# Block 0: the V product widened tile by tile and half by half, its weights in quarters, three Q and K slabs sent from ScalarE, two tiles turned by DMA

## The chip, the cores and the metric

One core of one Trainium2 chip. The views call its engines PE (matmuls), DVE (vector), ACT (ScalarE), POOL (GpSimd) and SP (SyncE, which here only sends DMAs). The metric is the time of one execution in microseconds of the device (us), the median of several executions. The kernel before takes 1619.12 us (3 runs, 1619.05 to 1619.46). The span given by a profile is usually 1.7 to 1.8 us shorter than the execution's time, so spans are compared with spans and times with times.

## The reference, cut to what matters

Two pairs of layers, each pair one attention layer over a sliding, dilated window and one gated feed-forward layer, on x of 2048 x 1024 in bf16:

```python
def _A_ref(x, wqkv, wo):                 # D = 1024, 32 heads
    qkv = (x @ wqkv)...                  # wqkv: 1024 x 3072, Q | K | V
    ...                                  # 8 keys at distance 2 per query, softmax
    return o... @ wo
x = x + _A_ref(_layernorm(x), A_wqkv, A_wo)
x = x + _B_ref(_layernorm(x), W_gate, W_up, W_down)     # and the same two lines once more
```

Only the first microseconds matter here: the layer norm of the first 512 tokens, called block 0 (four tiles of 128 tokens), and its product with the V weights, `v = layernorm(x) @ wqkv[:, 2048:3072]`.

## The kernel before

The kernel works in blocks of 512 tokens. It turns the normalised tokens before PE multiplies them, so that the 1024 features (8 chunks of 128, the contraction, `kc`) lie on partitions. For block 0 it does this on PE: a matmul with the identity into PSUM, then a copy. Loads go out from SyncE (queue q1) in program order; two x loads go out from ScalarE (queue q10).

```python
def load_x(b):
    for t in range(b * TPB, (b + 1) * TPB):
        if t == 0: ...                                   # half from SyncE, half from ScalarE
        elif t == 2: nc.scalar.dma_start(x_tiles[t][:], ...)
        else: sp_dma(x_tiles[t][:], ...)
load_x(0)                                                # all four x tiles, ahead of any weights

def want_v(key, mid, end):                               # V weights: two slabs of 1 MB, by output columns
    for g in range(2):
        want((key, g), wqkv_v[:, :, 2 * D + g * SLAB:2 * D + (g + 1) * SLAB], ...)

# ln_first(), its order of work, cut:
    bn(0, 0); bn(0, 1); aggr(0); ...                     # statistics of tile 0 on DVE
    apply(0); turn(0); apply(1)                          # turn: 8 transposes on PE
    copy(0, "a", 1); copy(0, "a", 0); turn(1); ...
    hold["later"] = {2: (lambda: (turn(2), copy(2, "a", 0), copy(2, "v", 1))),
                     4: (lambda: (turn(3), copy(3, "v", 0), copy(3, "a", 1)))}

def v_first(ln):                                         # V of block 0: two tiles at a time, whole contraction
    plan = [(c, 0, 2) for c in range(6)] + [(c, 2, 4) for c in range(6)] + [(c, 0, 4) for c in range(6, KC)]
    ...
            for kc in range(KC):
                mm(acc[:, cols], lhsT=slab[("v0", c // 4)][:, kc, ...], rhs=ln["xnT"][:, t0:t1, kc, :], ...)
            tail_act[0] = nc.scalar.copy(st["vT"][:, c, cols], acc[:, cols]).ins
            if i in ln["later"]: ln["later"][i]()        # tiles 2 and 3 turned on PE between products
```

The weights live in a ring of five slabs of 1 MB, so the sixth (the second half of K) can only be sent when the first V slab has been used up.

## Time and profile before

| | before |
|---|---|
| time, median | 1619.12 us |
| span of the profiled execution | 1617.5 us |
| PE busy, granted clock | 1608.1 us (99%), 1.00 |
| first V product starts | 9.83 us |
| first Q product starts (V is done) | 24.83 us |

The kernel is bound by PE from end to end; PE's only long wait is at the start. The chain of waits of the kernel before in its first 30 us (columns: start in us, length in us, what the end of the span hangs on at that time):

```profile
...
2.20 7.59 DMA w_v<-in_A_wqkv_dram
9.79 0.05 issue
9.83 2.79 PE acc_v L132 x24
12.63 0.45 PE tp L358 x8
13.07 1.75 PE acc_v L132 x16
14.82 0.45 PE tp L358 x8
15.27 9.57 PE acc_v L132 x72
24.83 1.73 PE acc_q L132 x8
...
```

Everything after 9.83 us is PE. The reader should see one DMA, the first V slab, issued at 2.20 and landed 7.59 us later, and then V without a gap, with two groups of eight transposes (0.45 us each) among the products.

PE's waits in the whole kernel before (columns: who waited for whom, us in total, times, longest):

```profile
...
PE scratch L132 <- DVE ones L290: 1.5, 1, 1.5
PE acc_v L132 <- DMA w_v<-in_A_wqkv_dram: 0.9, 1, 0.9
PE tp L358 <- DVE xn_first L106: 0.7, 1, 0.7
PE tp L358 <- DVE mean L106: 0.4, 1, 0.4
```

None of them comes after 9.83 us, and PE makes up 99% of the whole chain: every microsecond that PE idles later is counted as lost.

### The profile page before, as it was taken

How to read it: one execution, taken by the hardware profiler on the slowest of the kernel's cores; microseconds unless marked ns; L12 is line 12 of the kernel's file. 1: busy time of each engine (PE TensorE's matmuls, PEld its weight loads, DVE VectorE, ACT ScalarE, POOL GpSimd, SP SyncE). 2: the span in 40 equal slices, each digit the busy share in tenths (PEclk: the TensorE clock that was granted, in tenths of full speed). 3: DMA queues.
4: the chain of work that ended last, by engine and by line, in shares of the span. 5: the costliest groups of instructions: out<-in, count | busy, mean ns of one | idle time of the engine just before them, and what ended most of it. 6: DMA issues, size and time to landing. Idle time of an engine off the chain costs nothing.

```text
span 1617.5 us, 18722 instructions
## 1 busy us (share of the span) xinstructions
PE 1608.1 (99%) x7505; PEld 784.1 (48%) x7554; DVE 1138.3 (70%) x963; ACT 475.8 (29%) x971; POOL 176.1 (11%) x164
## 2 busy tenths in 40 slices
PE   9999999999999999999999999999999999999999
PEld 6646544444444445444454444544445444444444
DVE  6999979996989698929489293893939939311211
ACT  4853311131116313603136031361313311131110
POOL 2300100010003002300053000530005100000000
PEclk9999999999999999999999999999999999999999
DMA  9868867697669767794747948479574884755452
GB/s 295 184 197 251 213 173 244 182 213 206 209 189 216 202 183 216 188 248 144 229 160 202 240 152 230 153 203 254 160 231 155 207 240 156 209 171 167 155 169 66
DMA packets 408440, 317.92 MB, mean 197 GB/s; under 512 B 166432, under 2 KB 389024, under 8 KB 407840
## 3 DMA queue, kind: packets, MB, share of 16 engines
q1 hardware_dynamic: 407776, 316.13, 69.4%
q8 instruction: 59, 0.97, 0.2%
q10 hardware_dynamic: 576, 0.59, 0.1%
q14 instruction: 29, 0.24, 0.1%
HBM read 266.29 MB, written 34.66 MB: 186 GB/s over the span
## 4 chain that ended last, share of the span: by engine, by line
PE 99%; DMA 0%; issue 0%; SPq 0%; DVE 0%; DVEq 0%
PE acc_u L132 24%; PE acc_g L132 24%; PE dacc L132 18%; PE acc_v L132 7%; PE acc_q L132 7%; PE acc_k L132 7%; PE acc_wo L132 7%; PE dacc_pair L132 6%; DMA w_v<-in_A_wqkv_dram 0%; PE tp L358 0%; SPq L121 0%; PE L L132 0%; DVE x L778 0%; SPq L118 0%; DVEq L1017 0%
## 5 line engine op out<-in xcount | busy, mean ns | idle before, releaser
L132 PE MATMUL acc_g<-xnT_b,w_g 128*128 128x512 bf16 x1792 | 423.3, 379 | 0.0
L132 PE MATMUL acc_u<-xnT_b,w_u 128*128 128x512 bf16 x1792 | 423.3, 379 | 0.0
L731 ACT ACTIVATE r<-acc_g 128x512 bf16<-128x512 f32 x224 | 133.6, 596 | 728.7 <-PE acc_g L132 703.8
L106 DVE TENSOR_TENSOR hT<-acc_u,r 128x512 bf16<-128x512 f32 x224 | 151.0, 687 | 243.3 <-PE acc_u L132 240.8
L132 PE MATMUL dacc<-w_d,hT 128*128 128x512 bf16 (+1 forms) x1372 | 300.4, 375 | 1.5
L132 PEld LDWEIGHTS <-hT 128*128 128x128 bf16 x1820 | 178.1, 98 | 209.0
L132 PEld LDWEIGHTS <-w_g 128*128 128x128 bf16 x1792 | 175.4, 98 | 211.4
L132 PEld LDWEIGHTS <-w_u 128*128 128x128 bf16 x1792 | 175.3, 98 | 211.4
L106 DVE TENSOR_TENSOR pv<-a,vhm 128x4096 bf16<-128x4096 bf16 x64 | 143.6, 2285 | 0.0
L778 DVE TENSOR_TENSOR x<-dacc,x 128x512 bf16<-128x512 f32 (+1 forms) x38 | 24.5, 673 | 154.1 <-PE dacc L132 154.1
L549 DVE TENSOR_TENSOR t<-q,k 128x2048 f32<-128x2048 bf16 x56 | 128.0, 2292 | 6.7 <-ACT k L485 4.6
L106 DVE TENSOR_TENSOR t<-q,k 128x2048 f32<-128x2048 bf16 x56 | 127.5, 2287 | 3.9 <-ACT k L485 2.4
L106 DVE TENSOR_TENSOR pv<-pv 128x1024 bf16<-128x1024 bf16 (+1 forms) x128 | 113.8, 952 | 0.0
L132 PE MATMUL acc_wo<-w_o,oT 128*128 128x512 bf16 x498 | 111.1, 379 | 0.7
L249 POOL TENSOR_TENSOR st_b<-st_b,neg_half 128x1 f32<-128x1 f32 x29 | 43.8, 1517 | 609.9 <-ACT st_b L248 609.9
L562 DVE TENSOR_TENSOR ac<-ac,t 128x2048 f32<-128x2048 f32 x48 | 109.7, 2285 | 0.3
L106 DVE TENSOR_TENSOR ac<-ac,t 128x2048 f32<-128x2048 f32 x48 | 109.7, 2285 | 0.0
L490 POOL COPY kh<-k 128x14 bf16<-128x14 bf16 x40 | 53.7, 1348 | 506.5 <-ACT k L485 410.4
L132 PE MATMUL dacc_pair<-w_d,hT 128*128 128x512 bf16 x413 | 95.5, 379 | 0.4
L132 PEld LDWEIGHTS <-oT 128*128 128x128 bf16 x512 | 50.1, 98 | 60.4
L244 ACT ACTIVATE xn_b<-x 128x1024 bf16<-128x1024 bf16 x29 | 30.3, 1047 | 128.6 <-DVE x L106 66.5
L410 ACT CAST vT<-acc_v 128x512 bf16<-128x512 f32 x56 | 32.7, 586 | 54.0 <-PE acc_v L132 54.0
(131 smaller groups left out, 1226.8 us busy)
## 6 DMA issues: line engine op xcount, KB each, us to landing
w_g<-in_B_W_gate_dram SPq DMA_DIRECT2D x56, 1024.0 KB, 7.2
w_u<-in_B_W_up_dram SPq DMA_DIRECT2D x56, 1024.0 KB, 5.5
w_d<-in_B_W_down_dram SPq DMA_DIRECT2D x48, 1024.0 KB, 6.0
w_o<-in_A_wo_dram SPq DMA_DIRECT2D x16, 1024.0 KB, 6.6
vhm<-v_d SPq DMA_DIRECT2D x32, 284.0 KB, 6.7
v_d<-vT SPq DMA_DIRECT2D x8, 1024.0 KB, 9.0
oT<-o_d SPq DMA_DIRECT2D x32, 256.0 KB, 4.5
w_d<-in_B_W_down_dram SPq DMA_DIRECT2D x16, 512.0 KB, 3.7
```

The source lines that it names most:

```text
L106: tail_dve[0] = f(*args, **kwargs).ins
L132: tail_pe[0] = nc.tensor.matmul(*args, **kwargs).ins
L244: nc.scalar.activation(xn, xt[:], ACT.Square, accum_out=sq)
L249: nc.gpsimd.tensor_tensor(rstd, vpe, neg_half[:, 0:1], op=ALU.pow)
L410: tail_act[0] = nc.scalar.copy(st["vT"][:, c, :], acc[:]).ins
L490: nc.gpsimd.tensor_copy(khalo[n][:, c, :], k[:, BLK:BLK + HALO])
L549: nc.vector.tensor_tensor(t[:], i0, i1, op=ALU.mult)
L562: nc.vector.tensor_tensor(o, ac[:], t[:], op=ALU.add)
L731: tail_act[0] = nc.scalar.activation(rs[j][:], acc[:], ACT.Relu).ins
L778: run = dv if n < NB - 2 else (lambda f, *args, **kwargs: f(*args, **kwargs))
```

## The change

The intent is to start V earlier. V is widened tile by tile (first tile 0 alone, then tile 1) and its contraction is taken in two halves, so that the first products need only tile 0 and a quarter of the V weights. The V slabs are cut by contraction rows and each is sent as two DMAs of 512 KB; x tile 3 goes behind the first V slab. Three slabs of 1 MB go out from ScalarE: the first Q half (`act_slab("q", 0)`), the second Q half and the first K half. Tiles 2 and 3 are turned by DMA (SBUF to SBUF, issued by SyncE) instead of on PE, which also saves the PSUM copies. Smaller parts: the variance term goes from DVE to POOL, block 0 makes Q ahead of K by two groups, and the head sums move with it.

```diff
-    load_x(0)
+    load_x(0, range(TPB - 1))
...
+    def want_v_first(end0, end1):
+        for hh, end in enumerate((end0, end1)):
+            want(("v0", hh), qkv_half(2, hh), end)
...
+        if key[0] == "v0":
+            for i in range(2):
+                rows = slice(i * (KC // 4), (i + 1) * (KC // 4))
+                start(tv[:, rows, :], src[:, rows, :])
...
+    load_slab(("v0", 0), qkv_half(2, 0))
+    load_x(0, [TPB - 1])
+    load_slab(("v0", 1), qkv_half(2, 1))
...
+        def act_slab(nm, hh):
+            def start(dst, src):
+                on("a", nc.scalar.dma_start, dst, src)
+            load_slab(("qk01", nm, hh), qkv_half("qk".index(nm), hh), start)
+
+        def turn_dma(t):
+            return lambda: sp_dma(hold["xnT"][:, t, :, :], xna[:, t, :], True)
...
+        copy(0, "a", 0)
+        act_slab("q", 0)
...
+        def second():
+            turn(1)
+            apply(2)
+            copy(1, "v", 0)
+            copy(1, "v", 1)
+            act_square(3)
+            act_mean(3)
+            act_slab("q", 1)
+            act_slab("k", 0)
+            act_power(3)
+            apply(3)
...
-        hold["later"] = {2: (lambda: (turn(2), ...)), 4: (lambda: (turn(3), ...))}
+        hold["turns"] = [turn_dma(2), turn_dma(3)]
...
-        plan = [(c, 0, 2) for c in range(6)] + [(c, 2, 4) for c in range(6)] + [(c, 0, 4) for c in range(6, KC)]
+        tail = [(GRP * (2 + 4 * part + 0.5 * i), second_half(i, 2 * part)) for part in range(2) for i in range(KC // 2)]
+        return head, [(GRP, first_half(1)), (4 * GRP, first_half(2)), (5 * GRP, first_half(3))] + tail
...
-    ev.append((0.35, lambda: load_x(1)))
+    spread(ln_a[0]["turns"], 0.26, 0.01)
+    ev.append((0.35, lambda: load_x(1, [0, 1])))
+    ev.append((0.45, lambda: load_x(1, [2, 3])))
...
-    ev.append((t_v2 + 3.2 * GRP, lambda: head_mm(0)))
+    ev.append((t_v2 + 5.2 * GRP, lambda: head_mm(0)))
```

PE's order for V is now: tile 0, first half of the contraction; tile 1, first half; tiles 0 and 1, second half; then tile 2 and tile 3, first half; tiles 2 and 3, second half.

More of the change, by code (lines that the diff above doesn't have):

```diff
@@ L169, with load_x @@
         x_tiles.append(xt)
-    def load_x(b):
-        for t in range(b * TPB, (b + 1) * TPB):
+    def load_x(b, tiles=range(TPB)):
+        for t in (b * TPB + i for i in tiles):
             if t == 0:
@@ L192, in want_v, with qkv_half @@
             want((key, g), wqkv_v[:, :, 2 * D + g * SLAB:2 * D + (g + 1) * SLAB], mid if g == 0 else end)
+    def qkv_half(i, hh):
+        return wqkv_v[:, hh * (KC // 2):(hh + 1) * (KC // 2), i * D:(i + 1) * D]
+    def want_v_first(end0, end1):
+        for hh, end in enumerate((end0, end1)):
+            want(("v0", hh), qkv_half(2, hh), end)
     def want_qk(key, q_end, k_end):
@@ L196, in want_qk @@
             for hh in range(2):
-                want((key, nm, hh), wqkv_v[:, hh * (KC // 2):(hh + 1) * (KC // 2), i * D:(i + 1) * D], end)
+                want((key, nm, hh), qkv_half(i, hh), end)
     def want_wo(n, mid, end):
@@ L213, in want_down, with load_slab @@
             want(("d", n, half, s), wd_v[:, rows, half * SLAB:(half + 1) * SLAB], at + gap * min(8 * (s + 1), FC))
+    def load_slab(key, src, start=sp_dma):
+        shp = list(src.shape)
+        t = wring.tile([P, 8 * SLAB], BF16, tag="slab", name="w_" + "_".join(str(k) for k in key))
+        tv = t[:, 0:shp[1] * shp[2]].rearrange("p (a b) -> p a b", b=shp[2])
+        if key[0] == "v0":
+            for i in range(2):
+                rows = slice(i * (KC // 4), (i + 1) * (KC // 4))
+                start(tv[:, rows, :], src[:, rows, :])
+        else:
+            start(tv, src)
+        slab[key] = tv
     def slab_events(events):
         for i, (key, src, _) in enumerate(slab_plan):
-            def f(key=key, src=src):
-                shp = list(src.shape)
-                t = wring.tile([P, 8 * SLAB], BF16, tag="slab", name="w_" + "_".join(str(k) for k in key))
-                tv = t[:, 0:shp[1] * shp[2]].rearrange("p (a b) -> p a b", b=shp[2])
-                sp_dma(tv, src)
-                slab[key] = tv
+            if i < RING:
+                continue
             ends = sorted(end for _, _, end in slab_plan[:i])
-            events.append((ends[i - RING] + 0.3 if i >= RING else 0.1 * i, f))
+            events.append((ends[i - RING] + 0.3, lambda key=key, src=src: load_slab(key, src)))
     def ln_steps(n, which, early=False, dve=()):
@@ L313, in small @@
             return stat_pool.tile([P, 1], F32, tag="f" + name, name=name, bufs=bufs)
-        mean, vpe, rstd, bst = {}, {}, {}, {}
+        mean, rstd, bst, sq = {}, {}, {}, {}
         def bn(t, half):
@@ L324, in aggr @@
             on("v", nc.vector.bn_aggr, mv[:], bst[t][:].rearrange("p a b -> p (a b)"))
-            vpe[t], mean[t] = small("vpe1"), mv[:, 0:1]
-            on("v", nc.vector.tensor_scalar, vpe[t][:], mv[:, 1:2], EPS, None, op0=ALU.add)
-            power(t)
-        def power(t):
-            rstd[t] = small("rstd1")
-            on("g", nc.gpsimd.tensor_tensor, rstd[t][:], vpe[t][:], neg_half[:, 0:1], op=ALU.pow)
-        def act_stats(t):
-            st1 = stat_pool.tile([P, 2], F32, tag="st1", name="st1")
-            on("a", nc.scalar.activation, xna[:, t, :], x_tiles[t][:], ACT.Identity, accum_out=st1[:, 0:1])
-            on("a", nc.scalar.activation, xna[:, t, :], x_tiles[t][:], ACT.Square, accum_out=st1[:, 1:2])
-            return st1
@@ L339, in act_vpe, with power, act_square @@
-        def act_vpe(t, st1):
+            mean[t] = mv[:, 0:1]
+            power(t, mv[:, 1:2], 1.0)
+        def power(t, var, sign):
+            rstd[t], vpe = small("rstd1"), small("vpe1")
+            on("g", nc.gpsimd.tensor_scalar, vpe[:], var, sign, EPS, op0=ALU.mult, op1=ALU.add)
+            on("g", nc.gpsimd.tensor_tensor, rstd[t][:], vpe[:], neg_half[:, 0:1], op=ALU.pow)
+        def act_square(t):
+            sq[t] = small("sq1")
+            on("a", nc.scalar.activation, xna[:, t, :], x_tiles[t][:], ACT.Square, scale=float(D) ** -0.5,
+               accum_out=sq[t][:])
@@ L340, in act_vpe, with act_mean, act_power @@
+        def act_mean(t):
             mn = small("mean1")
-            on("v", nc.vector.tensor_scalar, mn[:], st1[:, 0:1], 1.0 / D, None, op0=ALU.mult)
+            on("a", nc.scalar.activation, xna[:, t, :], x_tiles[t][:], ACT.Identity, scale=1.0 / D, accum_out=mn[:])
+            mean[t] = mn[:]
+        def act_power(t):
             nvar = small("nvar1")
-            on("v", nc.vector.scalar_tensor_tensor, nvar[:], st1[:, 0:1], mn[:], st1[:, 1:2], op0=ALU.mult, op1=ALU.subtract)
-            vpe[t], mean[t] = small("vpe1"), mn[:]
@@ L345, in act_vpe, with apply @@
-            on("v", nc.vector.tensor_scalar, vpe[t][:], nvar[:], -1.0 / D, EPS, op0=ALU.mult, op1=ALU.add)
-            power(t)
-        def apply(t):
-            on("v", nc.vector.tensor_scalar, xna[:, t, :], x_tiles[t][:], mean[t], rstd[t][:],
+            on("v", nc.vector.scalar_tensor_tensor, nvar[:], mean[t], mean[t], sq[t][:], op0=ALU.mult, op1=ALU.subtract)
+            power(t, nvar[:], -1.0)
+        def apply(t, half=None):
+            cols = slice(0, D) if half is None else slice(half * SLAB, (half + 1) * SLAB)
+            on("v", nc.vector.tensor_scalar, xna[:, t, cols], x_tiles[t][:, cols], mean[t], rstd[t][:],
@@ L354, in turn @@
         def turn(t):
-            tps[t] = [psum.tile([P, KC // 2, P], BF16, tag="acc", name=f"tp{h}") for h in range(2)]
+            if t == 0:
+                tps[t] = [psum.tile([P, KC // 2, P], BF16, tag="acc", name=f"tp{h}")[:] for h in range(2)]
+            else:
+                both = psum_l.tile([P, 2, KC, P], BF16, tag="L", name="tp_pair")
+                tps[t] = [both[:, h, 0:KC // 2, :] for h in range(2)]
             for c in range(KC):
@@ L362, in copy @@
             f = nc.vector.tensor_copy if eng == "v" else nc.scalar.copy
-            on(eng, f, hold["xnT"][:, t, h * (KC // 2):(h + 1) * (KC // 2), :], tps[t][h][:])
+            on(eng, f, hold["xnT"][:, t, h * (KC // 2):(h + 1) * (KC // 2), :], tps[t][h])
+        def act_slab(nm, hh):
[4 more added lines that the diff above has]
+            return lambda: sp_dma(hold["xnT"][:, t, :, :], xna[:, t, :], True)
         warm = small("warm")
         on("a", nc.scalar.activation, warm[:], ones[:, 0:1], ACT.Identity)
-        scratch(14)
+        scratch(13)
         bn(0, 0)
@@ L370, in ln_first @@
         aggr(0)
+        act_square(2)
+        act_mean(2)
         bn(1, 0)
+        apply(0, 0)
+        apply(0, 1)
+        turn(0)
+        copy(0, "a", 0)
+        act_slab("q", 0)
         bn(1, 1)
         aggr(1)
-        st1 = act_stats(2)
-        apply(0)
-        turn(0)
-        apply(1)
-        copy(0, "a", 1)
-        copy(0, "a", 0)
-        turn(1)
-        act_vpe(2, st1)
-        copy(1, "v", 0)
-        copy(1, "a", 1)
-        bn(3, 0)
-        bn(3, 1)
-        apply(2)
-        aggr(3)
-        apply(3)
-        hold["later"] = {2: (lambda: (turn(2), copy(2, "a", 0), copy(2, "v", 1))),
-                         4: (lambda: (turn(3), copy(3, "v", 0), copy(3, "a", 1)))}
+        copy(0, "v", 1)
+        act_power(2)
+        apply(1, 0)
+        apply(1, 1)
+        def second():
[9 more added lines that the diff above has]
+            apply(3)
+        hold["second"], hold["last"] = second, last
+        hold["turns"] = [turn_dma(2), turn_dma(3)]
         return hold
@@ L416, in v_first @@
         st = att[0]
-        plan = [(c, 0, 2) for c in range(6)] + [(c, 2, 4) for c in range(6)] + [(c, 0, 4) for c in range(6, KC)]
-        def f_(i, c, t0, t1):
-            def f():
-                if i == 0:
-                    st["vT"] = big_tile([P, KC, BLK], "vT_0", True)
-                acc = psum.tile([P, BLK], F32, tag="acc", name="acc_v")
-                cols = slice(t0 * P, t1 * P)
-                with pe_group():
-                    for kc in range(KC):
-                        mm(acc[:, cols], lhsT=slab[("v0", c // 4)][:, kc, (c % 4) * P:(c % 4 + 1) * P],
-                           rhs=ln["xnT"][:, t0:t1, kc, :], start=(kc == 0), stop=(kc == KC - 1))
-                tail_act[0] = nc.scalar.copy(st["vT"][:, c, cols], acc[:, cols]).ins
-                if i in ln["later"]:
-                    ln["later"][i]()
-            return f
@@ L434, in v_first, with prod @@
-        at, out = 0.0, []
-        for i, (c, t0, t1) in enumerate(plan):
-            out.append((at, f_(i, c, t0, t1)))
-            at += GRP * (t1 - t0) / TPB
-        return out
+        pairs, opened = {}, set()
+        def prod(kc, c, t0, t1):
+            part = t0 // 2
+            if (part, c // 2) not in pairs:
+                pairs[part, c // 2] = psum.tile([P, 2, BLK // 2], F32, tag="acc", name="acc_v")
+            acc = pairs[part, c // 2][:, c % 2, (t0 % 2) * P:(t0 % 2 + t1 - t0) * P]
+            with pe_group():
+                mm(acc, lhsT=slab["v0", kc // (KC // 2)][:, kc % (KC // 2), c * P:(c + 1) * P],
+                   rhs=ln["xnT"][:, t0:t1, kc, :], start=(part, c // 2) not in opened, stop=(kc == KC - 1),
+                   skip_group_check=True)
+            opened.add((part, c // 2))
@@ new lines, in head, with first_half, second_half, f @@
+        def head():
+            st["vT"] = big_tile([P, KC, BLK], "vT_0", True)
+            for kc in range(KC // 2):
+                if kc == KC // 2 - 1:
+                    ln["second"]()
+                for c in range(KC):
+                    prod(kc, c, 0, 1)
+        def first_half(t):
+            def f():
+                for c in range(KC):
+                    for kc in range(KC // 2):
+                        prod(kc, c, t, t + 1)
+            return f
+        def second_half(i, t0):
+            def f():
+                for c in (2 * i, 2 * i + 1):
+                    for kc in range(KC // 2, KC):
+                        prod(kc, c, t0, t0 + 2)
+                tail_act[0] = nc.scalar.copy(st["vT"][:, 2 * i:2 * i + 2, t0 * P:(t0 + 2) * P],
+                                             pairs.pop((t0 // 2, i))[:]).ins
+            return f
@@ L447 @@
     khalo = {}
-    QK_FIRST = [(nm, c) for c in range(KC) for nm in ("q", "k")]
+    QK_STAGED = [(nm, c) for c in range(KC) for nm in ("q", "k")]
     QK_ORDER = [("q", 0), ("q", 1)]
@@ L486, in f @@
                     if b == 0:
-                        nc.gpsimd.memset(k[:, 0:HALO], 0.0)
+                        with (tc.issue_after(ln["last"]["g"]) if "last" in ln else nullcontext()):
+                            nc.gpsimd.memset(k[:, 0:HALO], 0.0)
                     else:
@@ L504, in get @@
             return f
-        order = QK_FIRST if n < NB else QK_ORDER
+        order = QK_STAGED if staged else QK_ORDER
         steps = [f_(nm, c) for nm, c in order]
@@ L855 @@
     t_gu0 = t_fill + GRP * (4 * KC - ahead)
-    want_v("v0", t_v0 + GRP * 5, t_qk0)
+    want_v_first(t_v0 + GRP * 6, t_qk0)
     want_qk("qk01", t_qk1 + GRP * KC, t_v1)
@@ L861 @@
     want_wo(0, t_fill, t_fill)
-    for at, f in v_first(ln_a[0]):
-        ev.append((t_v0 + at, f))
-    ev.append((0.35, lambda: load_x(1)))
-    ev.append((t_v0 + GRP * 5 + 0.6, lambda: load_x(2)))
-    ev.append((t_v0 + GRP * 5 + 0.7, zero_v))
+    head, steps = v_first(ln_a[0])
+    place(steps, t_v0)
+    ev.append((0.25, head))
+    spread(ln_a[0]["turns"], 0.26, 0.01)
+    ev.append((0.35, lambda: load_x(1, [0, 1])))
+    ev.append((0.45, lambda: load_x(1, [2, 3])))
+    ev.append((t_v0 + GRP * 6 + 0.6, lambda: load_x(2)))
+    ev.append((t_v0 + GRP * 6 + 0.7, zero_v))
     stats, apply, turn, ln_a[1] = ln_steps(1, "a", True, range(TPB))
@@ L874 @@
     spread(qk_steps(0, ln_a[0], "qk01"), t_qk0, GRP)
-    spread(prod_sum_steps(0), t_qk0 + 3.5, 4.4)
+    spread(prod_sum_steps(0), t_qk0 + GRP * K_STEP[0] + 1.8, 4.4)
     spread(load_v_steps(0), t_qk0 + 19.0, 1.0)
@@ L885 @@
     spread(v_steps(2, ln_a[2], "v123", True), t_v2, GRP)
-    ev.append((t_v2 + 3.2 * GRP, lambda: head_mm(0)))
-    spread(softmax_steps(0), t_v2 + 3.3 * GRP, 0.01)
-    t_pv0 = t_v2 + 2.2 * GRP + 10.0
+    ev.append((t_v2 + 5.2 * GRP, lambda: head_mm(0)))
+    spread(softmax_steps(0), t_v2 + 5.3 * GRP, 0.01)
+    t_pv0 = t_v2 + 4.2 * GRP + 10.0
     spread(pv_steps(0), t_pv0, 4.3)
```

## The prediction

> **What bounds the kernel.** The page gives PE busy 1608.1 of 1617.5 us (99%), granted clock 1.00; the chain of waits is 99% PE. From 9.83 us on, the waits view lists no PE wait. Only the head can give: the chain's one long non-PE piece is 7.59 us for the first V slab (issued 2.20, landed 9.79). V of block 0 then runs from 9.83 to 24.83 us without a gap, two transpose groups (0.45 us each) among it. So about 2 us can be won.
>
> **What the change does, costed.**
> 1. Head DMA. Before, V waits for 1 MB of x plus 1 MB of V; now a 0.5 MB quarter and tile 0 suffice. Summing the bandwidth row of the DMA view, the first quarter lands near 6.5 us, the second near 7.8, the last near 12. V then waits for tile 0.
> 2. Tile 0: its statistics end at 5.03 us. Two POOL instructions (a power takes 0.55 to 0.79 us) give rstd near 6.3; half an apply (0.3 us), transposes and a copy (0.59 us, behind ACT's tile 2 passes, ending near 7.4) let V start near 8.1: 1.7 us earlier.
> 3. V on PE: 128 matmuls of 128 columns at 0.056 us (as the transposes), 64 of 256 at 0.109 us and one transpose group make 14.6 us, against 15.0.
> 4. New waits. Tile 1 runs through POOL twice and through DVE behind the apply of tile 2: I expect about 1 us of PE idle between the head and tile 1's first half. Tiles 2 and 3 turn by DMA. A DMA transpose of one tile landed here 3.1 to 3.8 us after issue in a quiet stretch, 8 us in a loaded one. Applied near 10.9 and 13.8 us, they land near 15.5 and 18.5; PE wants them near 16.6 and 18.4. I allow 0.4 us of stall.
> 5. Q and first K slabs go out from ScalarE. [...] Here one Q slab held SyncE 3.2 us. The risk is the same hold on ScalarE, delaying tile 3.
>
> V should end near 24.0 instead of 24.83.
>
> **Further on.** Block 0's Q/K order changes: the first K comes two groups (3.45 us) later relative to PE, so DVE, nearly full from 38 to 210 us, runs that much later relative to PE. The tightest place is the first gate product: its last DMA transpose landed at 187.5 us, PE began at 191.08, slack 3.6 us. That is all but used up; I allow 0.2 us. After 230 us DVE has idle time.
>
> **Sum.** -1.7 (start) -0.4 (PE work) +1.0 (tile 1) +0.4 (DMA transposes) +0.2 (gate) gives -0.5 us if all waits come, about -2.1 if none does. I put it at -1.4 us: 1617.7 us, range 1616.1 to 1619.5. Faster by over 2%: 0.3%; within: 99.2%; slower: 0.5%.
>
> **What would show it.** The first acc_v matmul near 8.1 us, released by the ACT copy of tile 0, not by DMA; 16 transposes on PE instead of 32; PE idle before tile 1's matmuls, released by DVE; first acc_q near 24 us; little PE idle at the first acc_g.
>
> **What would make it wrong.** ScalarE held for microseconds by its slab issues, so that tile 3 lands after 20 us (up to 2 us slower); Q slabs slowing the second V half; a gate stall of 1 to 2 us; or POOL and DVE waits that overlap better than I assume (1616).

## The result

| | before | after |
|---|---|---|
| time, median of 6 | 1619.09 us (1618.84 to 1619.46) | 1625.49 us (1624.42 to 1627.45) |
| span of the profiled execution | 1617.5 us | 1623.4 us |
| first V product | 9.83 us | 7.88 us |
| PE idle in V | 0 | 6.05 us |
| first Q product | 24.83 us | 30.88 us |

The ratio is 1.0040, 95% interval 1.0027 to 1.0053. A ratio here is the mean time of one kernel's fast runs over that of the other's of the same rounds, so not quite the ratio of the medians quoted. It is slower by 6.4 us without doubt, outside the predicted range, and its runs scatter over 3 us where those of before scatter over 0.6.

The chain of waits after the change, first microseconds, columns as above:

```profile
...
9.47 0.55 DVE xn_first L106
...
10.04 11.80 DMA xnT_first<-xn_first
...
21.89 8.98 PE acc_v L132 x96
30.88 5.18 PE acc_q L132 x24
36.06 1.73 PE acc_k L132 x8
...
```

V begins early, but now the end of the kernel hangs on one DMA transpose: tile 2, issued at 10.04 us, landed at 21.85. PE's waits say the same:

```profile
...
PE acc_v L132 <- DMA xnT_first<-xn_first: 6.0, 1, 6.0
PE scratch L132 <- DVE ones L309: 1.5, 1, 1.5
PE acc_v L132 <- ACT xnT_first L327: 0.6, 1, 0.6
PE tp L382 <- DVE xn_first L106: 0.2, 1, 0.2
```

The wait for the V weights has gone, as intended, and 6.0 us of waiting for `xnT_first` has come. There is a second loss behind it. Stretches of the kernel after (columns: the stretch in us, its length, busy us and number of instructions of each engine, then the granted PE clock, DMA share, GB/s):

```profile
...
7.88:15.84 7.96, 7.83 (x104) 7.08 (x103) 2.86 (x9) 4.05 (x7) 2.10 (x7) 1.00 1.13 366
15.84:21.89 6.05, 0.00 (x1) 0.00 (x1) 0.00 (x0) 0.58 (x1) 0.00 (x0) 0.74 1.00 304
21.89:25.60 3.71, 3.71 (x35) 3.71 (x36) 2.19 (x6) 0.00 (x0) 0.46 (x1) 0.50 0.82 292
25.60:30.88 5.28, 5.28 (x64) 4.92 (x63) 5.07 (x15) 1.76 (x3) 1.65 (x3) 1.00 0.43 116
...
```

After the wait PE ran 3.71 us at a clock of 0.50. Half of that, 1.85 us, is lost beside the wait itself. The trace's clock record puts the half clock from 18.77 to 25.59 us.

The sum, to the first Q product: start 1.95 us earlier; wait +6.05; half clock +1.85; the products themselves 7.96 + 8.98 - 1.85 = 15.09 us against 15.00, +0.09. Together +6.04, and the first Q product is at 30.88 against 24.83, +6.05. From there on nothing more is lost: the span grew by 5.9.

What the two queues did meanwhile. The DMA view of the kernel after from 17 to 20 us (queue; packets; MB; share of the 16 engines' time):

```profile
...
DMA packets 1024, 1.14 MB, mean 381 GB/s; under 512 B 530, under 2 KB 530, under 8 KB 1024
...
q10 hardware_dynamic: 510, 1.01, 88.6%
q1 hardware_dynamic: 514, 0.13, 19.3%
...
```

On q10 are the Q and K slabs, in packets of 2 KB; on q1 is the transpose, in packets of 256 B (the trace records each packet's size). 510 packets against 514: in these 3 us the two queues moved as many packets each, and so the transpose got 0.13 of 1.14 MB. That they take turns packet by packet was my reading of these two counts, and my first theory of the cause.

### The profile page after: what moved, and what is told of

It reads as the page before. It is cut to its first block, busy times and chain, and to the rows that moved or that the text cites. A ratio compares the mean times of both kernels' runs of the same rounds, so it can differ in the third digit from the quotient of the medians.

```text
span 1623.4 us, 18849 instructions
## 1 busy us (share of the span) xinstructions
PE 1609.0 (99%) x7568; PEld 787.1 (48%) x7617; DVE 1136.5 (70%) x958; ACT 474.3 (29%) x965; POOL 181.9 (11%) x168
## 4 chain that ended last, share of the span: by engine, by line
PE 98%; DMA 1%; DVE 0%; issue 0%; POOL 0%; DVEq 0%
PE acc_u L132 24%; PE acc_g L132 24%; PE dacc L132 18%; PE acc_k L132 7%; PE acc_q L132 7%; PE acc_wo L132 7%; PE acc_v L132 7%; PE dacc_pair L132 6%; DMA xnT_first<-xn_first 1%; DMA x<-in_A_x_dram 0%; POOL rstd L327 0%; DVE xn_first L106 0%; DVE bst L106 0%; DVE bst L103 0%; PE L L132 0%
```

## The experiments

Theory A: the transposes are starved by a second queue whose packets are eight times as large. Theory B: a DMA transpose is slow here for its own reasons, or behind the V weights on its own queue. Theory C: what counts is the bytes in flight ahead of it, in whichever queue. A fourth possibility was that another wait stood behind this one. "T2" and "T3" are the DMA transposes of tiles 2 and 3; `turns` in the diffs is the list of what SyncE sends after the V weights. All twelve kernels gave the reference's result.

| run | median us | before, same rounds | T2: issued, landed after | T3: issued, landed after |
|---|---|---|---|---|
| the change | 1625.49 | 1619.09 | 10.0, 11.8 | 13.1, 9.5 |
| e1_turn_pe | 1619.34 | 1619.24 | on PE | on PE |
| e2_slabs_sp | 1622.42 | 1619.24 | 10.0, 4.5 | 15.0, 3.1 |
| e3_slabs_1k | 1624.31 | 1619.24 | 10.1, 11.0 | 13.1, 11.1 |
| e4_fill | 1623.84 | 1619.24 | 10.2, 11.9 | 13.2, 9.7 |
| e5_q0_ahead | 1618.73 | 1619.25 | 9.9, 7.3 | 13.8, 4.5 |
| e6_q0_act | 1619.07 | 1619.25 | 10.1, 6.8 | 13.2, 4.6 |
| e7_pe_sp | 1618.64 | 1619.25 | on PE | on PE |
| e1b_turn_pe | 1618.97 | 1619.25 | on PE | on PE |
| e8_turns_first | 1621.33 | 1619.29 | 9.9, 3.3 | 13.8, 3.1 |
| e9_no_early_slab | 1623.84 | 1619.29 | 10.0, 3.5 | 14.1, 8.0 |
| e10_x_late | 1626.61 | 1619.29 | 10.2, 10.4 | 13.5, 10.9 |
| e11_q0_between | 1619.04 | 1618.97 | 10.1, 5.1 | 12.9, 6.5 |

### e1_turn_pe: tiles 2 and 3 on PE again

```diff
-        hold["turns"] = [turn_dma(2), turn_dma(3)]
+        hold["late"] = {0: lambda: late_turn(2), 2: lambda: late_turn(3)}   # turn(t); copies on DVE
+        hold["turns"] = []
...
+                if t0 == 0 and i in ln["late"]:          # after a pair of second-half products
+                    ln["late"][i]()
```

> The change with tiles 2 and 3 turned on PE again (16 transposes, copies on DVE), all else as changed. If the wait for the DMA transposes is the whole loss: no PE wait above 0.3 us after 7.9 us, clock 1.00, V from 7.9 to about 23.9 us (15.1 us of products plus 0.9 us of transposes), time near 1618.2 us, 7.3 below the changed kernel. If another wait was hidden behind it (slabs late through sharing, gate late because DVE now runs 3.45 us later relative to PE): PE idles elsewhere and the time stays above 1619.1.

Measured 1619.34 us (4 runs, 1619.03 to 1619.69), 6.1 below the changed kernel. The chain of waits of its profiled execution:

```profile
...
10.51 2.82 PE acc_v L132 x40
13.33 0.45 PE tp_pair L382 x8
13.77 1.75 PE acc_v L132 x16
15.52 0.45 PE tp_pair L382 x8
15.97 7.94 PE acc_v L132 x104
23.91 5.18 PE acc_q L132 x24
...
```

V ends at 23.91 us as computed, no PE wait after the first product (7.96 us) is above 0.2 us, and that execution spanned 1616.6 us, 0.9 less than before. So, in this trace, the DMA transposes are the whole loss and no other wait stands behind them; the fourth possibility falls. But that execution's time was all the same 1619.57 us, and the three others spanned 1617.3 to 1617.7 against 1617.2 to 1617.6 of before. So the time is that of before, the expected 1618.2 was missed, and why the others took longer has no trace here (e1b, below, explains a part).

### e2_slabs_sp: the three slabs on SyncE, behind the transposes

```diff
-        act_slab("q", 0)
-            act_slab("q", 1)
-            act_slab("k", 0)
-        hold["turns"] = [turn_dma(2), turn_dma(3)]
+        hold["turns"] = [turn_dma(2), turn_dma(3), sp_slab("q", 0), sp_slab("q", 1), sp_slab("k", 0)]
```

> The change with the three Q/K slabs sent from SyncE behind the two DMA transposes instead of from ScalarE. Theory A (256 B packets of the transposes take turns packet by packet with 2 KB packets of the slabs on the other queue): with no second queue the transposes land 3.1 to 4.5 us after issue, near 14 and 17 us; PE waits under 0.5 us; V ends near 23.0, Q slabs land near 22.5, time near 1617.3 us. Theory B (a DMA transpose is this slow here by itself, or behind the V weights on its own queue): tile 2 still lands after 19 us, PE waits over 3 us, time above 1621.

Measured 1622.42 us (1620.57 to 1622.65). T2 landed 4.5 us after issue and T3 3.1, against 11.8 and 9.5, and PE waited for neither: theory B falls. The time was a miss all the same, for two reasons that PE's waits show:

```profile
...
PE acc_k L132 <- DMA w_qk_k<-in_A_wqkv_dram: 3.7, 1, 3.7
PE acc_v L132 <- DMA w_v<-in_A_wqkv_dram: 2.0, 2, 1.7
...
```

The last K half now stood on the one queue behind everything (3.7 us), and in this execution the first two V quarters landed late (waits of 1.7 and 0.3 us).

### e3_slabs_1k: the ScalarE slabs in rows of 1 KB

```diff
-                on("a", nc.scalar.dma_start, dst, src)
+                for i in range(2):
+                    cols = slice(i * SLAB, (i + 1) * SLAB)
+                    on("a", nc.scalar.dma_start, dst[:, :, cols], src[:, :, cols])
```

> The change with each ScalarE slab sent as two halves with rows of 1 KB instead of 2 KB: same bytes, same queue, half the packet size. Theory A (turns by packet): while both queues run, the transposes move about 80 KB/us instead of 43, tile 2 lands near 18.5 to 19.5 us instead of 21.85, time 3 to 5 us below the changed kernel (about 1621 to 1622.5). Theory C (what matters is the bytes in flight, or turns by byte): tile 2 lands at 21.5 us or later and the time does not fall. Theory B: no change either.

Measured 1624.31 us (1623.36 and 1625.26), T2 landed at 21.08. The expected time and landing were missed, though the split between the queues moved as theory A said. The DMA view of this run from 18 to 21 us:

```profile
...
DMA packets 1486, 0.83 MB, mean 278 GB/s; under 512 B 880, under 2 KB 1486, under 8 KB 1486
...
q10 hardware_dynamic: 623, 0.62, 76.9%
q1 hardware_dynamic: 863, 0.21, 41.3%
...
```

The transposes' part of the bytes rose from 0.13 of 1.14 MB to 0.21 of 0.83. But 863 packets against 623 are not equal turns: from 18.75 us on q10 moved fewer packets. The stretch in which both queues were full, from 17.25 to 18.75 us, is the cleaner one:

```profile
...
q10 hardware_dynamic: 416, 0.42, 80.9%
q1 hardware_dynamic: 428, 0.11, 33.1%
...
```

The packets are again nearly equal in number, and the transposes moved 0.11 MB in 1.5 us, 73 KB/us against 43 in the changed kernel (80 were expected). So in these two traces the split goes with the packet size, and theory C's turns by byte fall. But from 18 to 21 us all traffic together was 278 GB/s, against 381 in the changed kernel from 17 to 20. Turn-taking alone does not give the landing time. Something else was missing.

### e4_fill: PE kept busy in the wait

```diff
                                              pairs.pop((t0 // 2, i))[:]).ins
+                if t0 == 0 and i == KC // 2 - 1:
+                    scratch(23)                          # 23 matmuls on constants, about 5 us
```

> The change with 23 matmuls of 512 columns on constants (about 5 us at full clock) put into the PE wait before tile 2; nothing else. If 1.9 us of the loss is the PE clock at half after the wait: the clock stays 1.00, the rest of V takes 7.1 us instead of 8.98, time near 1623.6 us. If those products were slow for another reason (late tile 3, memory shared with the DMA): still about 9 us, time unchanged at 1625.5.

Measured 1623.84 us (4 runs, three within 1623.67 to 1623.97, one 1628.75, which was not traced). The stretches before, in and after the wait:

```profile
...
15.84:22.14 6.30, 5.16 (x25) 2.28 (x24) 0.00 (x0) 0.59 (x1) 0.00 (x0) 1.00 0.96 287
22.14:29.37 7.23, 7.23 (x97) 6.86 (x97) 5.54 (x14) 1.76 (x3) 1.57 (x3) 1.00 0.74 234
...
```

T2 landed no earlier, but the clock stayed at 1.00 and the rest of V took 7.23 us instead of 8.98: 1.75 us. The clock term is confirmed by itself.

### e10_x_late: a control

In the next runs the last K half goes ahead of two x loads, to mend e2's K wait. This run has only that.

```diff
-    ev.append((0.45, lambda: load_x(1, [2, 3])))
+    ev.append((t_v0 + GRP * 6 + 0.4, lambda: load_x(1, [2, 3])))
```

> Control: the changed kernel with only the order of the last K half and two x loads changed, as in the runs with slabs moved. It should do nothing for the wait: tile 2 lands near 21.8 us, clock halves after the wait, time 1624 to 1627 as the changed kernel. If it falls by 1 us or more, part of those runs' gain was this order.

Measured 1626.61 us (1624.99 and 1628.23). T2 landed 10.4 us and T3 10.9 us after issue, and the half clock returned. So this order mends nothing, and what the next runs gain is not its doing.

### e6_q0_act: only the first Q half from ScalarE

```diff
-            act_slab("q", 1)
-            act_slab("k", 0)
-        hold["turns"] = [turn_dma(2), turn_dma(3)]
+        hold["turns"] = [turn_dma(2), turn_dma(3), sp_slab("q", 1), sp_slab("k", 0)]
```

> Only the first Q half (1 MB, issued near 7 us) stays on ScalarE; the other two slabs go on SyncE behind the transposes. Theory A as a dose: the second queue holds 1 MB instead of 3, so it is drained near 13.5 us and the transposes run free after that: tile 2 lands near 15, tile 3 near 17.5, PE waits under 0.5 us, time 1617.0 to 1618.6. If the late first packet of tile 2 (4.0 us after issue in the changed kernel, 1.2 in the run with all on SyncE) came from the two ScalarE slabs issued 0.1 and 0.5 us after it, its first packet now comes before 12 us; if it came from the second queue being busy at all, near 13.5.

Measured 1619.07 us (5 runs, 1618.53 to 1619.34), the loss gone but for 0.9 us of PE waiting:

```profile
...
PE acc_v L132 <- DMA xnT_first<-xn_first: 0.9, 1, 0.9
PE acc_v L132 <- ACT xnT_first L327: 0.7, 1, 0.7
...
```

T2's first packet moved at 13.1 us, not before 12. So the late first packet was not the doing of the slabs issued after it (in e10, which has them as the changed kernel has, it came at 13.2). In the packet records, that first packet comes as the slab issued before it, on the other queue, runs out (its packets thin out in the half microsecond from 13.0). In the changed kernel the 16 packets of 4 B that come on q10 at the end of the same slab lie between 13.10 and 13.84 us, and T2's first packet at 14.1.

### e9_no_early_slab: no slab from ScalarE ahead of T2

```diff
-        act_slab("q", 0)
-        hold["turns"] = [turn_dma(2), turn_dma(3)]
+        hold["turns"] = [turn_dma(2), turn_dma(3), sp_slab("q", 0)]
```

> The change without the early ScalarE slab: the first Q half goes on SyncE behind the transposes, the other two slabs stay on ScalarE, issued 0.1 and 0.5 us after tile 2's transpose. This parts the two halves of the delay. If the late first packet (14.0 us in the changed kernel) was the wait for the slab issued before it on the other queue, tile 2's first packet now comes near 11.3 us. If turn-taking then holds whenever both queues have packets, tile 2 or at the latest tile 3 crawls at about 43 KB/us until the 2 MB are through (near 18 us), and tile 3 lands near 18 to 19; time 1618 to 1621. If only issue order mattered, tile 2 lands near 14 with no slab packet before its end.

Measured 1623.84 us (1623.61 and 1624.08). T2 now moved from 11.3 us on and landed 3.5 us after issue. T3, issued at 14.05 us with 2 MB of slabs on ScalarE issued before it, took 8.0 us. The DMA view in T3's wait, from 13.4 us to 18.0:

```profile
...
DMA packets 828, 1.68 MB, mean 365 GB/s; under 512 B 16, under 2 KB 16, under 8 KB 827
...
q10 hardware_dynamic: 827, 1.66, 101.6%
q8 instruction: 1, 0.02, 1.4%
...
```

There is no q1 line at all: from T3's issue at 14.05 us not one of its packets moved until 18.2 us, when the slabs were nearly through (the 16 packets under 512 B are among q10's 827). So the delay has two halves, and this run parts them. First, the transposes on q1 got nothing until the slab traffic that was issued before them on q10 was nearly done: T2 until 14.1 us in the changed kernel, T3 until 18.2 us here. Then, where slabs issued later had packets by that time, both queues moved, in equal numbers of packets (514 to 510 in the changed kernel). Of what was expected, the first half held; the crawl of T3 at 43 KB/us did not come, a full stop came in its place; and the time was over the expected 1621: PE waited 3.9 us for T3, and then ran at half clock from 23.10 to 26.51 us.

The wait for a first packet was not the transposes' alone. The first Q slab, a plain load, was issued on q10 at 6.95 us in the changed kernel. The DMA view from 7 to 10.2 us has no line for q10:

```profile
...
DMA packets 673, 1.28 MB, mean 401 GB/s; under 512 B 47, under 2 KB 47, under 8 KB 673
...
q1 hardware_dynamic: 673, 1.28, 104.5%
...
```

Its first packet moved at 10.48 us, 3.5 us after issue, as the V weights issued before it on q1 ran out. In e1 the same slab was issued at 7.05 us and first moved at 10.72; from there on it shared the engines with the x loads on q1.

### e5_q0_ahead: the early slab on the same queue

```diff
-        hold["turns"] = [turn_dma(2), turn_dma(3)]         # and no act_slab
+        hold["turns"] = [sp_slab("q", 0), turn_dma(2), turn_dma(3), sp_slab("q", 1), sp_slab("k", 0)]
```

> All slabs on SyncE again, but one of them (1 MB, first Q half) placed ahead of the two DMA transposes on the same queue, and the last K half ahead of two x loads. Theory A (the loss is the turn-taking with a second queue): on one queue the transposes just follow the slab: tile 2's packets start near 14 us and run at 150 KB/us or more, landing near 16 us and tile 3 near 18; PE waits under 1 us for them; V ends near 23.3 us, no K wait as in the run before; time 1617.0 to 1618.6. Theory C (bytes in flight ahead of the transposes matter, whichever queue): landing 18 us or later, PE waits 2 us or more.

Measured 1618.73 us (5 runs, 1618.24 to 1619.81). T2's packets started near 13.5 us, as expected, right behind the slab, but it landed at 17.28 instead of 16, and PE waited 1.3 us. The same MB ahead of T2 costs about the same on q1 (7.3 us to landing) as on q10 (6.8 us, e6). As far as the first packet goes, theory C is thus right in these runs: it was what had been issued before that counted, on either queue. What the ScalarE queue added in the changed kernel is the second half, slabs issued after T2 that moved packet for packet with it. In the 1.3 us too much all traffic nearly stopped (1, 9 and 45 GB/s in the three slices from 16.0 to 17.2 us); such stops are told next.

### e7_pe_sp and e1b_turn_pe: PE transposes again

e7 is e1 with the three slabs on SyncE as well (and the two x loads later, as in e10); e1b is e1 once more.

```diff
-        act_slab("q", 0)                                  # e7 only, and "q" 1 and "k" 0
+        hold["turns"] = [sp_slab("q", 0), sp_slab("q", 1), sp_slab("k", 0)]
```

> Tiles 2 and 3 turned on PE and the three slabs on SyncE (no slab on ScalarE at all). If sending slabs from ScalarE is in itself worth nothing, same as the kernel with PE transposes and ScalarE slabs: V ends near 23.9 us, time within 0.5 us of it in the same rounds. If the ScalarE issues help or cost by themselves, V or the first Q products move by 0.5 us or more.

> The same kernel as e1_turn_pe, for more times and a second trace: its profiled execution spanned 0.9 us less than before, its other executions 0 to 0.2 us less. Theory: V now starts when the first V quarter lands, and that varies by up to 2 us from run to run (6.6 us in one trace, 8.8 in another), while before a later landing hid it. Then this trace, if longer than 1616.6, shows the first product later than 7.96 us, released by the DMA of the V weights; the mean time is 1618.5 to 1619.4. If it starts at 7.96 again and the span is longer, the loss is elsewhere.

Measured 1618.64 us (1618.26 to 1619.00) and 1618.97 us (1618.61 to 1620.27). They lie 0.33 us apart, within the 0.5 expected: with the transposes on PE, sending the slabs from ScalarE was worth nothing. e1b's profiled execution spanned 1617.3 us. V started at 7.95 us as in e1, so my theory of a late first quarter fails here. What was late is the last V quarter, issued at 3.83 us and landed 9.13 us later, with PE waiting 0.32 us for it. Early landings of the weights do vary from run to run (the last V quarter landed at 12.2 us in the changed kernel and at 12.96 here), and a start at 7.9 us leaves no room for that, but only part of e1b's 0.7 us is explained so.

The stops show in the changed kernel beside e1. In both views a packet of 16 KB goes by on queue q8, whose kind the trace calls `instruction`; I call it the program fetch. The DMA view of the changed kernel from 14 to 17 us, and then of e1_turn_pe (the GB/s of 40 slices):

```profile
...
GB/s 355 335 314 358 440 365 341 614 307 427 348 335 396 338 399 341 365 276 150 150 61 58 0 0 3 27 0 0 31 0 0 31 0 31 492 300 236 447 492 492
...
q8 instruction: 1, 0.02, 2.3%
...
```

```profile
...
GB/s 382 410 410 355 437 410 437 382 328 355 410 601 382 410 382 355 382 300 355 410 410 410 301 383 355 437 382 355 410 328 382 437 410 328 382 410 410 410 382 410
...
q8 instruction: 1, 0.02, 2.3%
...
```

In both the fetch is one packet of 1.1 us (from 14.56 and from 14.83 us). In the changed kernel, with a transpose in flight, all queues together fell to 61 GB/s or less for 14 slices, about a microsecond, and 15 slab packets are recorded as taking 0.95 to 1.35 us, where the median is 0.08; in e1, with plain traffic alone, no slice falls below 300. But a stop does not need the fetch: in e9 all traffic together was 58 GB/s from 12.0 to 12.5 us with T2 in flight, and that run's fetch came at 13.50; in e10 it was 33 GB/s from 14.0 to 14.5 us, with the fetch at 15.55.

### e8_turns_first and e11_q0_between: two better orders

```diff
-        hold["turns"] = [turn_dma(2), turn_dma(3)]         # and no act_slab, as in e2
+        hold["turns"] = [turn_dma(2), turn_dma(3), sp_slab("q", 0), sp_slab("q", 1), sp_slab("k", 0)]  # e8
+        hold["turns"] = [turn_dma(2), sp_slab("q", 0), turn_dma(3), sp_slab("q", 1), sp_slab("k", 0)]  # e11
```

> As the earlier run with all slabs on SyncE behind both DMA transposes, but the last K half now ahead of two x loads. That run's 3.7 us wait for K was the FIFO of one queue: here it should fall below 0.7 us. Tile 2 lands near 14, tile 3 near 17 us, both before PE wants them; V ends near 23.0 (24 in an execution with a late V quarter); time 1617.2 to 1618.7, the best of all so far. If K is still late by 2 us or more, the FIFO explanation of that wait is wrong.

> Best order tried from what the runs showed: one queue, first Q half between the two DMA transposes, so that it fills the 2 us in which the queue had nothing to move (13 to 15 us) and K comes 2 us earlier than with both transposes first. Tile 2 lands near 13.5 us, tile 3 near 17.5 (PE wants it near 17.6), V ends at 22.9 to 23.6, K wait under 0.5 us; time 1617.2 to 1618.6, below before in every round. Rival: the stops that come with each DMA transpose (about 1 us of no traffic) take the same time again wherever the slab stands; then tile 3 lands after 18.5 or K waits over 1 us and the time is 1618.6 or more.

e8: 1621.33 us (5 runs, 1620.11 to 1621.85). Both transposes landed within 3.3 us of issue, PE's timeline has the first Q product at 22.91 us, the earliest of all, and then PE waited 2.2 us for the last K half, against 3.7 in e2. By what I had written before the run, 2 us or more speaks against the order on the queue as the cause. The order was a part of it: that half landed at 31.23 us against 34.01 in e2, but PE asked for it 1.2 us earlier, so that the wait shrank by 1.5 us only. For the rest, from 17.5 us until that half landed at 31.2 the queue moved 370 to 410 KB in every microsecond, about as much as all plain traffic together in e1 (391 GB/s from 12 to 20 us), so I take it as full: with the Q slabs held back until both transposes were through, four slabs of 1 MB had to follow at once. Not all of its 5.35 MB were slabs: two x loads (0.5 MB) still stood ahead of that half and landed at 27.85 and 28.52 us, and an order without them was not tried.

e11: 1619.04 us (5 runs, 1618.33 to 1619.75), before 1618.97 in the same rounds. The K wait was gone, but T2 landed at 15.19 us instead of 13.5 and T3 at 19.38 instead of 17.5:

```profile
...
PE acc_v L132 <- DMA xnT_first<-xn_first: 1.6, 1, 1.6
...
PE acc_v L132 <- ACT xnT_first L327: 0.5, 1, 0.5
```

The rival's landing came true (T3 after 18.5 us): what the order wins, the later landings of the transposes take back. That stops caused them here was not shown. None of the versions beats the kernel before by more than about 0.6 us; the interval of each of e5, e6, e7 and e11 includes 1.

## Why the prediction was wrong

It said 1617.7 us, 1616.1 to 1619.5; it was 1625.49.

- **Head DMA and tile 0 (steps 1 and 2): right.** The V quarters landed at 6.6, 8.3, 10.3 and 12.2 us in the changed kernel (predicted 6.5, 7.8, last 12), and V started at 7.88 us (predicted 8.1), released by the copy on ACT.
- **PE work (step 3): too good.** Predicted 14.6 us, measured 15.09. Between the first V product and the last there is one transpose group now, where there were two, but without them the products take 14.64 us instead of 14.10: the smaller products cost more than the group saved.
- **Tile 1 (step 4, first half): wrong, harmless.** I allowed 1.0 us; PE did not idle at all between tile 0 and tile 1. I had no duration for the variance term on POOL and took about that of the power. It took 0.19 us.
- **DMA transposes (step 4, second half): the step that failed.** "Applied near 10.9 and 13.8 us, they land near 15.5 and 18.5 ... I allow 0.4 us of stall." They were applied even earlier (10.0 and 13.1 us) and landed at 21.85 and 22.6: 6.05 us of PE idle. The mechanism of a wait for a loaded DMA was named, but the term was mis-sized fifteenfold. By the packet records tile 2's 11.8 us were 4.1 us until its first packet (1.3 in e2, with no slab ahead), 6.6 us in which its 1024 packets took turns with the slabs, about 1 us of that nearly stopped, and 1.1 us more until it had landed. I took a landing time between a quiet and a loaded stretch of the trace of before, where all of that traffic was on one queue, and did not ask what the three slabs of step 5 would do on a second one. e1, which takes the DMA transposes away, and e6, which takes two of the slabs away, each remove the loss.
- **Slabs from ScalarE (step 5): the right place, the wrong danger.** I feared that ScalarE would be held by its issues. They took it 0.4 to 0.5 us each. The damage was in the DMA traffic: from 17 to 20 us the slabs' packets on q10 took 88.6% of the 16 DMA engines' time and the transpose's on q1 19.3%, in nearly equal numbers (510 and 514). That sending from another engine changes nothing but who spends the issue time was an assumption of mine that no trace of the kernel before had shown, and I did not multiply by the packet sizes, 256 B and 2 KB.
- **The clock: missing.** The prediction has no term for it. In the changed kernel the clock was 0.50 from 18.77 to 25.59 us; at 18.77 PE had been idle for 2.93 us (from 15.84). In e9 a wait of 3.9 us was followed by half clock from 23.10 to 26.51 us, and in e8 one of 2.2 us was enough (31.81 to 35.22 us), while in e2 one of 3.7 us was followed by none. The cost was 1.85 us by the windows, 1.75 by e4. A wait of that length should be priced at more than its length, though not by a sharp rule.
- **The gate: right within its size.** The last transpose for the first gate product landed at 195.8 us, PE began at 197.1: the slack shrank from 3.6 to 1.3 us, and PE did not wait. I had written 0.2 us.

What stays open. Why the transposes got no packet until slabs issued before them on the other queue were nearly done (13.1, 14.1 and 18.2 us in three runs), and why the plain first Q slab waited in the same way for the V weights (10.48 us), while in e1 plain loads on the two queues shared the engines from 10.72 us on. And why all traffic nearly stopped for about a microsecond with a transpose in flight (from 15.5 to 16.55 us in the changed kernel): no run tests a cause. The scatter of the changed kernel's times over 3 us was not traced either.

## What to carry to other kernels

Work moved off the bottleneck engine onto DMA has to be priced in the traffic that will be there when it runs, by packet size and by what is issued before and after it on every queue, not by its landing time in a quiet stretch: here the same transpose landed 3.3 us after issue in e8 and 11.8 us in the changed kernel. Where PE had no other gap, a start 1.95 us earlier was worth little unless everything behind it came earlier too: here Q, K and the turned tiles were all due at the same time from the same 16 engines, and every order that was tried gave back nearly all that the start had won. And PE waits of some 2 to 6 us could cost more than their own length: PE ran at half clock for 3.4 us in e8 and for 3.7 us after the wait in the changed kernel (in e2 not at all).
